# Fewer PE instructions, larger weight loads, one store, and one load split by partition halves in a cached-attention and GEGLU kernel

## The chip, the cores and the metric

The kernel runs on one core of one Trainium2 chip. The metric is the device time of one execution in microseconds (us), the median of several. One execution of one experiment (e17) was in a slower state, 209.65 us against 191.32 to 191.49 for the other three of that kernel; all times compared below are of fast executions. Where 2% is called faster, same or slower, fast runs alone are used, with a 95% interval.

## The reference

A single token per sequence (B = 2, D = 640) goes through a layer norm with a modulation computed from `c`, attention of 32 heads of 192 over the last 1024 of 4096 cached keys, and a GEGLU feed-forward of width 1536. All arrays are bf16.

```python
mod = (silu(c) @ w_mod).reshape(2, 6, 1, 640)          # sa, ca, ga, sb, cb, gb
h = layernorm(x) * (1 + ca) + sa
q = (h @ wq).reshape(B, 1, 32, 192)                    # wq 640 x 6144
k, v = k_cache[:, :, 3072:], v_cache[:, :, 3072:]      # B x 32 x 1024 x 192 each
x = x + ga * (softmax(q @ k.T * 192**-0.5) @ v).reshape(B, 1, 6144) @ wo
h = layernorm(x) * (1 + cb) + sb
x = x + gb * ((gelu(h @ w_gate) * (h @ w_up)) @ w_down)  # w_down 1536 x 640
```

## The kernel before

It is a stream of loads: nearly 77 MB pass through SBUF once, and compute follows. `w_mod` comes first, then `wq`, the key and value groups and `wo` through a ring of eight slots; then `w_gate`, `w_up` and `w_down` go into the place where `w_mod` was. All large loads are issued by SyncE on one queue (`q1` of the page below, 76.88 MB). The parts that matter here are the score reduction, the tail's loads, the feed-forward and the end.

```python
KPS = SLOT // NQ                        # wq in 5 pieces of one k-tile
WD_SPLIT = [(0, 2), (2, 1), (3, 1)]     # w_down in 3 pieces
# ... score reduction: 12 chunks of 16 columns, N = 256 each
for t in range(NCH):
    last = e.matmul(o_ap, lhsT=ident_b[:, :], rhs=prod[:, pz, :, t * GC:(t + 1) * GC], ...)
# ... the loads of the tail
S.dma("sp", k_dma(wg_v..., B_w_gate...), sem_wg, ...)
S.dma("sp", k_dma(wu_v..., B_w_up...), sem_wu, ...)
wd_src = B_w_down.rearrange("(a p r) n -> p a (r n)", a=FA, r=FR)
for ci, (a0, na) in enumerate(WD_SPLIT):
    S.dma("sp", k_dma(wd_v[:, a0 * FR:(a0 + na) * FR, :]..., wd_src[:, a0:a0 + na, :]), sem_wd[ci], ...)
# ... gate and up: the weights are the stationary operand, 60 matmuls of 2 columns each
for fc in range(FC):
    for k in range(KT):
        last = e.matmul(ps[:, bk, fc * 2:fc * 2 + 2], lhsT=wv[:, k, ...][:, :, r], rhs=h2T[:, k, :], ...)
# ... down, one function per piece of w_down; then the end
for b in range(B):
    S.dma(("sp", "act")[b], k_dma(out[b, 0, :]..., finb[b:P:32, :]), sem_out[b], ...)
with nc.Block() as block:
    ...                                 # each engine's list is emitted inside the block
```

Of the kernel before, what the change touches and what calls it, by code (L numbers as in the profile page):

```python
# [5 lines left out]
ALU = mybir.AluOpType  # L6
# [8 lines left out]
class _Op:  # L15
    __slots__ = ("eng", "fn", "name", "deps", "sem", "val", "inc")

    def __init__(self, eng, fn, name):
        self.eng = eng
        self.fn = fn  # L20
        self.name = name
        self.deps = []
        self.sem = None
        self.val = None
        self.inc = 1


class _Sched:

    def __init__(self, nc, es):  # L30
        self.nc = nc
        self.es = es
        self.lists = {k: [] for k in _COMPUTE + ("sp",)}
        self.counter = {k: es.enter_context(nc.semaphore("cnt_" + k)) for k in _COMPUTE}
        self.bufs = {}
        self.dma_uses = {}
        self.ncount = {k: 0 for k in _COMPUTE}

# [20 lines left out]
    def op(self, eng, fn, reads=(), writes=(), name="", deps=()):  # L59
        o = _Op(eng, fn, name)  # L60
        self._track(o, reads, writes, deps)
        self.lists[eng].append(o)
        self.ncount[eng] += 1
        o.sem = self.counter[eng]
        o.val = self.ncount[eng]
        return o

    def dma(self, eng, fn, sem, reads=(), writes=(), name="", deps=()):
# [7 lines left out]
        self.lists[eng].append(o)  # L76
        return o

    def emit(self, engname, eng, tail=None):
        waited = {}  # L80
        cnt = 0
        for o in self.lists[engname]:
            need = {}
            for d in o.deps:
                if d.eng == "pe" and engname == "pe" and d.inc == 1:
                    continue
                key = d.sem.num
                if need.get(key, (None, 0))[1] < d.val:
                    need[key] = (d.sem, d.val)
            for key, (s, v) in need.items():  # L90
                if waited.get(key, 0) >= v:
                    continue
                eng.wait_ge(s, v)
                waited[key] = v
# [9 lines left out]
def bass_adaLN_cond__sliding_block_cached__geglu_ffn__decode_kernel(  # L104
# [31 lines left out]
    FA, FR = 4, 3  # L136
    FC = F // P
    assert B == 2 and D == KT * P and J * PH == W and NQD * HQ == H and NT * P == NQ
    assert DD * NT == Dh and DD * H == P and FA * FR == FC and FC * P == F and DR == KT * 32
# [5 lines left out]
    GC = 512 // J  # L145
# [7 lines left out]
    KPS = SLOT // NQ  # L153
    NWQ = -(-KT // KPS)
    TPS = SLOT // D
    WO_SPLIT = []
    while sum(n for _, n in WO_SPLIT) < NT:
        t0 = sum(n for _, n in WO_SPLIT)
        WO_SPLIT.append((t0, min(TPS, NT - t0)))
    NWO = len(WO_SPLIT)  # L160
    WD_SPLIT = [(0, 2), (2, 1), (3, 1)]
    X0 = HQ * DD * (NQD - 1) + DD - 1
    ZW = X0 + P + 1
    QW = 2 * Dh
    NQB = NQ // (NR * QW)
    MH = 3 * DR

    es = ExitStack()
    with es:
# [11 lines left out]
        qbc = sb("qbc", [P, B, NQD, Dh], BF16)  # L181
# [6 lines left out]
        mneg = sb("mneg", [P, HQ], BF16)  # L188
# [8 lines left out]
        scT = sb("scT", [P, KT, B], BF16)  # L197
# [16 lines left out]
        nmx = sb("nmx", [1, 2, HQ], F32)  # L214
# [3 lines left out]
        On = sb("On", [P, 2, ON], BF16)  # L218
        oT = sb("oT", [P, NT, B], BF16)
        gl = sb("gl", [P, FC, B], F32)  # L220
        aT = sb("aT", [P, FC, B], BF16)
# [14 lines left out]
        sem_x = [S.sem("d_x%d" % b) for b in range(B)]  # L236
# [3 lines left out]
        sem_wu = S.sem("d_wu")  # L240
        sem_wd = [S.sem("d_wd%d" % i) for i in range(len(WD_SPLIT))]
        sem_ring = [S.sem("d_ring%d" % i) for i in range(NS)]
        sem_out = [S.sem("d_out%d" % b) for b in range(B)]
# [10 lines left out]
        slot_of = {it: n % NS for n, it in enumerate(items)}  # L254
        ring_state = {"next": 0, "done": set()}

# [3 lines left out]
        def ring_src(it):  # L260
            kind, i = it
            if kind == "wq":
                k0, k1 = i * KPS, min(KT, (i + 1) * KPS)
                return A_wq.rearrange("(p k) n -> p (k n)", k=KT)[:, k0 * NQ:k1 * NQ], (k1 - k0) * NQ
# [5 lines left out]
            return src[b, quad * HQ:(quad + 1) * HQ, K0:Sk, :].rearrange("h (p j) d -> p h (j d)", p=PH), SLOT  # L270

        def declare_ring(consumed=()):
            ring_state["done"].update(consumed)
            while ring_state["next"] < len(items):
                n = ring_state["next"]
                if n >= NS and items[n - NS] not in ring_state["done"]:
                    break
                slot = n % NS
                src, width = ring_src(items[n])
                S.dma("sp", k_dma(ring[:, slot, 0:width], src), sem_ring[slot], writes=[("ring", slot)], name="ld_%s%d" % items[n])  # L280
# [7 lines left out]
        xz = S.bufs["xr"][0]  # L288
        for b in range(B):
            S.dma("act", k_dma(xr[b:P:32, :], A_x[b, 0, :].rearrange("(i n) -> i n", i=NR)), sem_x[b], writes=[("xr", b)], deps=[xz], name="ld_x%d" % b)  # L290
# [8 lines left out]
        S.op("pool", lambda e: e.affine_select(out=selrow[:, :, :], in_=ones_b[:, 0:1].unsqueeze(2).broadcast_to([P, NR, B]),  # L299
                                                pattern=[[-32, NR], [-1, B]],  # L300
                                                compare_op=ALU.is_equal, fill=0.0, base=0, channel_multiplier=1),
             reads=["ones_b"], writes=["selrow"], name="selrow")
# [11 lines left out]
        S.op("pool", lambda e: e.memset(zsel[:, :, :], 0.0), writes=["zsel"], name="zsel0")  # L314

# [13 lines left out]
        def c_T(e):  # L329
            last = None  # L330
            for j in range(KT):
# [3 lines left out]
        S.op("act", lambda e: e.activation(out=scT[:, :, :], in_=c_ps[:, :, :], func=ACTF.Silu),  # L335
             reads=[bank(BK_T)], writes=["scT"], name="silu")
        S.op("dve", lambda e: e.tensor_copy(out=X[:, :], in_=xr[:, :]),
             reads=["xr"] + [("xr", b) for b in range(B)], writes=["X"], name="x_f32")
# [20 lines left out]
        def ln_mod(tag, opc_idx, s_idx, dst_bf):  # L359
# [7 lines left out]
            def f(e):  # L367
# [12 lines left out]
        S.op("dve", lambda e: e.tensor_scalar(out=mneg[:, :], in0=mask_h[:, :], scalar1=-1.0, scalar2=NEG, op0=ALU.add, op1=ALU.mult),  # L380
             reads=["mask_h"], writes=["mneg"], name="mneg")
# [3 lines left out]
        S.op("dve", lambda e: e.tensor_reduce(out=zsel[:, :, X0:X0 + DD * HQ].rearrange("p q (h d) -> p q h d", d=DD)[:, :, :, 0],  # L385
# [4 lines left out]
        for half in range(2):  # L390
            def f(e, half=half):
                last = None
                for k in range(KT):
                    wv = wm_v[:, k, :].rearrange("p (m i n) -> p m i n", i=NR, n=DR)
                    for i in range(NR):
                        last = e.matmul(ps[32 * i:32 * i + B, half, 0:MH].rearrange("p (m n) -> p m n", n=DR), lhsT=scT[:, k, :],  # L396
# [11 lines left out]

        for w in range(NWQ):
            def f(e, w=w):  # L410
                last = None
                for k in range(w * KPS, min(KT, (w + 1) * KPS)):
                    wv = ring[:, slot_of[("wq", w)], (k - w * KPS) * NQ:(k - w * KPS + 1) * NQ].rearrange("p (q h d) -> p q h d", h=NR, d=Dh)
                    for n in range(NQB):
                        for i in range(NR):
                            last = e.matmul(ps[32 * i:32 * i + B, n, 0:QW].rearrange("p (q d) -> p q d", d=Dh), lhsT=hT[:, k, :],  # L416
                                            rhs=wv[:, 2 * n:2 * n + 2, i, :],
                                            start=(k == 0), stop=(k == KT - 1), tile_position=(0, 32 * i))
                return last
            S.op("pe", f, reads=["ln1_out", ("ring", slot_of[("wq", w)])], writes=[bank(n) for n in range(NQB)], name="q1_%d" % w)  # L420
            declare_ring([("wq", w)])
        for n in range(NQB):
            if n % 2 == 0:
                S.op("act", lambda e, n=n: e.activation(out=qrow[:, n * QW:(n + 1) * QW], in_=ps[:, n, 0:QW], func=ACTF.Copy),
                     reads=[bank(n)], writes=[("qrow", n)], name="q1_evac%d" % n)
            else:
                S.op("dve", lambda e, n=n: e.tensor_copy(out=qrow[:, n * QW:(n + 1) * QW], in_=ps[:, n, 0:QW]),  # L427
                     reads=[bank(n)], writes=[("qrow", n)], name="q1_evac%d" % n)
        for u, (n, b) in enumerate((n, b) for n in range(NQB) for b in range(B)):
            bk = BK_T + u % 4  # L430
            S.op("pe", lambda e, n=n, b=b, bk=bk: e.matmul(ps[:, bk, 0:QW], lhsT=selq[:, b, :], rhs=qrow[:, n * QW:(n + 1) * QW], start=True, stop=True),
                 reads=[("selq", b), ("qrow", n)], writes=[bank(bk)], name="q2_%d_%d" % (n, b))
            S.op("act", lambda e, n=n, b=b, bk=bk: e.activation(out=qbc[:, b, 2 * n:2 * n + 2, :].rearrange("p q d -> p (q d)"),  # L433
                                                                in_=ps[:, bk, 0:QW], func=ACTF.Copy),
                 reads=[bank(bk)], writes=[("qbc", b, 2 * n), ("qbc", b, 2 * n + 1)], name="q2_evac%d_%d" % (n, b))
        S.op("dve", lambda e: e.memset(ps[:, 5:8, :], 0.0), writes=[bank(k) for k in range(5, 8)], name="init_O2")  # L436

        def d_mul(g, ci):
# [4 lines left out]
                                                  in1=qbc[:, b, quad, :].unsqueeze(1).broadcast_to([P, JC, Dh]), op=ALU.mult),  # L443
                 reads=[("ring", sl), ("qbc", b, quad)], writes=[("prod", 2 * (g % 2) + ci)], name="mul%d_%d" % (g, ci))

        def p_reduce(g, ci):
            bk = g % 2
            pz = 2 * (g % 2) + ci

            def f(e):  # L450
                last = None
                o_ap = ps[:, bk, ci * JC * GC:(ci + 1) * JC * GC].rearrange("p (j c) -> p j c", c=GC)
                for t in range(NCH):
                    last = e.matmul(o_ap, lhsT=ident_b[:, :], rhs=prod[:, pz, :, t * GC:(t + 1) * GC],  # L454
                                    start=(ci == 0 and t == 0), stop=(t == NCH - 1), skip_group_check=True)
                return last
            S.op("pe", f, reads=[("prod", 2 * (g % 2) + ci), "ident_b"], writes=[bank(bk)], name="red%d_%d" % (g, ci))

        def c_sum(g):
            z = g % 2  # L460
            S.op("dve", lambda e: e.tensor_reduce(out=S_sb[:, z, :], in_=ps[:, z, :].rearrange("p (j c) -> p j c", c=GC),  # L461
                                                  axis=AX.X, op=ALU.add),
                 reads=[bank(z)], writes=[("S", z)], name="sum_%d" % g)
# [5 lines left out]
        def c_max2(g):  # L469
            z = g % 2  # L470
            S.op("dve", lambda e: e.tensor_reduce(out=nmx[:, z, :], in_=ps[0:1, BK_T, 0:P].rearrange("p (x h) -> p h x", h=HQ),  # L471
                                                  axis=AX.X, op=ALU.max, negate=True),
                 reads=[bank(BK_T)], writes=[("nmx", z)], name="max2_%d" % g)

        def c_bc(g):
            z = g % 2

            def f(e):
                o_ap = ps[:, BK_T, P:P + HQ]
                e.matmul(o_ap, lhsT=ones_f[0:1, :], rhs=nmx[:, z, :], start=True, stop=False)  # L480
                return e.matmul(o_ap, lhsT=ident_b[:, :], rhs=mneg[:, :], start=False, stop=True)  # L481
# [207 lines left out]
```

## Time and profile before

| | before |
|---|---|
| time, median of 3 runs | 192.12 us |
| span of the profiled run | 190.5 us |
| bytes loaded | 76.88 MB |
| PE matmuls | 1401 |
| 16 KB instruction fetches in the DMA records | 11 |

The page's busy line and its slices say what bounds the kernel. PE is TensorE with its matmuls, PEld its weight loads, DVE is VectorE, ACT ScalarE, POOL GpSimd; x counts instructions. A digit is the busy share of one of 40 slices in tenths; the last line is what the DMA engines moved.

```profile
PE 109.4 (57%) x1401; PEld 74.3 (39%) x1401; DVE 88.7 (47%) x147; ACT 29.2 (15%) x74; POOL 3.0 (2%) x14
...
DMA  7999999999999999999999999999999999999960
GB/s 259 388 416 441 423 427 428 418 436 426 418 429 426 421 427 425 421 428 424 423 426 431 418 423 434 419 421 431 428 416 434 420 423 424 426 421 432 399 252 8
...
q1 hardware_dynamic: 7192, 76.88, 96.0%
q8 instruction: 11, 0.18, 0.4%
```

No compute engine is busy over 57%; the load queue is busy 96.0% of the time that 16 engines have, at 416 to 441 GB/s from the third slice to the 37th. So in the body the DMA rate alone counts, and most of what is left to gain lies in the head and the tail. The `q8` line is easily overlooked: these are the fetches of instructions (11 of 16 KB), and the profile counts them on the same 16 engines.

Next the windows of the tail. The columns are the window in us and its length, then the busy time (and count) of PE, PEld, DVE, ACT and POOL, the granted PE clock, the DMA share of the 16 engines, and GB/s.

```profile
178.00:180.00 2.00, 1.76 (x60) 1.73 (x60) 0.17 (x1) 0.00 (x0) 0.00 (x0) 0.50 0.95 392
180.00:182.00 2.00, 0.27 (x9) 0.22 (x8) 0.00 (x0) 0.19 (x1) 0.00 (x0) 0.50 1.04 410
182.00:183.00 1.00, 1.00 (x43) 1.00 (x41) 0.00 (x0) 0.00 (x0) 0.00 (x0) 0.50 0.92 361
183.00:184.00 1.00, 0.60 (x22) 0.51 (x19) 0.18 (x1) 0.00 (x0) 0.00 (x0) 0.50 0.63 257
184.00:185.00 1.00, 0.43 (x16) 0.46 (x20) 0.00 (x0) 0.00 (x0) 0.00 (x0) 0.50 0.30 123
185.00:186.00 1.00, 0.89 (x30) 0.42 (x20) 0.00 (x0) 0.00 (x0) 0.00 (x0) 0.50 0.19 66
186.00:187.00 1.00, 0.40 (x16) 0.19 (x12) 0.00 (x0) 0.00 (x0) 0.00 (x0) 0.50 0.02 8
```

The share falls from 0.92 to 0.02 over five windows: the 16 engines don't end together. The last load has 16 completions in the records. The records carry no engine numbers; a completion is read here as one engine's. The first comes at 183.13 and the last at 186.77, a spread of 3.64 us. Work of the kernel's end waits for the slowest engine, as the end of the chain of waits shows (start in us, duration, what):

```profile
156.72 30.05 DMA r<-in_B_w_down_dram
186.77 0.04 issue
186.81 0.60 PE ps L625 x12
187.41 0.02 issue
187.44 0.33 DVE fin L630
```

After the last piece of `w_down` only 12 matmuls, two DVE operations and the store are left.

### The profile page before, as it was taken

The page shows a single profiled execution, that of the slowest core. Times are in us where ns is not written, and L with a number is a line of the kernel's source. Part 1 is how long each engine was busy: PE and PEld are TensorE (multiplying, and loading weights), DVE is VectorE, ACT ScalarE, POOL GpSimd, SP SyncE. Part 2 cuts the span into 40 slices and gives each one's busy share as a digit, 9 for nine tenths or more (in the row PEclk, how much of TensorE's full clock was granted, in tenths as well). Part 3 has the DMA queues.
Part 4 walks back from the last instruction along what each step waited for, and adds up shares of the span by engine and source line. Part 5 has one row for each costly group of instructions (what it writes and reads, how often), then busy time and mean ns, then how long its engine had stood idle before and what let it go on. Part 6 is the DMA issues. An engine that isn't in the chain of part 4 may idle for free.

```text
span 190.5 us, 3243 instructions
## 1 busy us (share of the span) xinstructions
PE 109.4 (57%) x1401; PEld 74.3 (39%) x1401; DVE 88.7 (47%) x147; ACT 29.2 (15%) x74; POOL 3.0 (2%) x14
## 2 busy tenths in 40 slices
PE   0014853628678773674689656646759856224452
PEld 0011310105556552462457444434536624223450
DVE  6123000248699549458477476485495620003201
ACT  3031100370022101011011011012010230003400
POOL 6000000000000000000000000000000000000000
PEclk9999999999999999999957999999975995555555
DMA  7999999999999999999999999999999999999960
GB/s 259 388 416 441 423 427 428 418 436 426 418 429 426 421 427 425 421 428 424 423 426 431 418 423 434 419 421 431 428 416 434 420 423 424 426 421 432 399 252 8
DMA packets 7234, 77.09 MB, mean 405 GB/s; under 512 B 818, under 2 KB 820, under 8 KB 1460
## 3 DMA queue, kind: packets, MB, share of 16 engines
q1 hardware_dynamic: 7192, 76.88, 96.0%
q8 instruction: 11, 0.18, 0.4%
q14 instruction: 3, 0.02, 0.0%
q10 hardware_dynamic: 28, 0.01, 0.0%
HBM read 76.88 MB, written 0.00 MB: 404 GB/s over the span
## 4 chain that ended last, share of the span: by engine, by line
DMA 71%; DVE 13%; SPq 5%; PE 4%; issue 3%; ACT 2%
DMA ring<-in_A_k_cache_dram 39%; DMA ring<-in_A_wq_dram 16%; DMA r<-in_B_w_down_dram 16%; DVE prod L441 8%; SPq L246 5%; PE ps L454 3%; DVE S_sb L461 2%; ACT qbc L433 2%; PE ps L416 1%; DVE ps L436 1%; DVE M L464 1%; PE ps L480 0%; DVE rden L516 0%; PE ps L625 0%; DVE Sb_sb L486 0%
## 5 line engine op out<-in xcount | busy, mean ns | idle before, releaser
L441 DVE TENSOR_TENSOR prod<-ring,qbc 128x3072 bf16<-128x3072 bf16 x32 | 55.9, 1752 | 21.7 <-DMA ring<-in_A_k_cache_dram 21.7
L454 PE MATMUL ps<-prod,ident_b 128*128 128x256 bf16 x384 | 53.4, 296 | 21.0 <-DVE prod L441 21.0
L454 PEld LDWEIGHTS ps<-prod,ident_b 128*128 128x128 bf16 x384 | 38.2, 105 | 33.1 <-DVE prod L441 25.4
L518 ACT ACTIVATE On<-ps,rden 128x384 bf16<-128x384 f32 x16 | 9.3, 580 | 46.5 <-DVE rden L516 33.1
L480 PE MATMUL ps<-nmx,ones_f 1*128 1x4 f32 x32 | 6.5, 271 | 15.2 <-DVE nmx L471 15.2
L506 PE MATMUL ps<-ring,E_sb 128*8 128x384 bf16 x256 | 13.6, 334 | 0.0
L489 ACT ACTIVATE E_sb<-Sb_sb 128x128 bf16<-128x128 f32 x16 | 5.0, 309 | 53.3 <-DVE Sb_sb L486 53.3
L480 PEld LDWEIGHTS ps<-nmx,ones_f 1*128 1x128 f32 x32 | 5.1, 198 | 20.3 <-DVE nmx L471 20.3
L575 PE MATMUL ps<-ring,oT 128*2 128x160 bf16 x192 | 7.2, 333 | 8.3 <-DMA ring<-in_A_wo_dram 7.8
L461 DVE TENSOR_REDUCE S_sb<-ps 128x32 f32<-128x512 f32 x16 | 10.8, 673 | 1.7 <-PE ps L454 1.7
L416 PE MATMUL ps<-ring,hT 128*2 128x384 bf16 x80 | 7.1, 516 | 7.5 <-DMA ring<-in_A_wq_dram 6.7
L486 DVE TENSOR_TENSOR Sb_sb<-S_sb,ps 128x128 f32<-128x128 f32 x16 | 4.6, 288 | 10.7 <-PE ps L481 10.7
L575 PEld LDWEIGHTS ps<-ring,oT 128*2 128x2 bf16 x192 | 5.4, 115 | 9.9 <-DMA ring<-in_A_wo_dram 9.3
L592 DVE TENSOR_TENSOR lnt<-ps,modR 128x160 f32<-128x160 f32 x1 | 0.3, 324 | 17.5 <-PE ps L575 17.5
L345 PE MATMUL ps<-st,selstat 128*128 128x2 f32 x4 | 1.1, 349 | 11.2 <-ACT sqj L341 11.2
L427 DVE CAST qrow<-ps 128x384 bf16<-128x384 f32 x2 | 1.0, 553 | 13.7 <-PE ps L416 13.7
L416 PEld LDWEIGHTS ps<-ring,hT 128*2 128x2 bf16 x80 | 2.1, 108 | 12.6 <-DMA ring<-in_A_wq_dram 8.9
L530 PEld LDWEIGHTS ps<-On,zsel 128*128 128x128 bf16 x128 | 6.1, 110 | 1.2 <-ACT On L518 1.2
L530 PE MATMUL ps<-On,zsel 128*128 128x48 bf16 x128 | 6.0, 187 | 0.8 <-ACT On L518 0.8
L506 PEld LDWEIGHTS ps<-ring,E_sb 128*8 128x8 bf16 x256 | 4.9, 86 | 3.0 <-issue 0.5
L495 PEld LDWEIGHTS ps<-denp,maskc 128*128 128x128 f32 x32 | 5.3, 209 | 1.2 <-ACT E_sb L489 1.0
L396 PE MATMUL ps<-r,scT 128*2 128x480 bf16 x40 | 4.3, 596 | 2.1 <-DMA r<-in_w_mod_dram 2.1
(71 smaller groups left out, 74.9 us busy)
## 6 DMA issues: line engine op xcount, KB each, us to landing
ring<-in_A_k_cache_dram SPq DMA_DIRECT2D x16, 1536.0 KB, 25.1
ring<-in_A_v_cache_dram SPq DMA_DIRECT2D x16, 1536.0 KB, 25.6
ring<-in_A_wq_dram SPq DMA_DIRECT2D x5, 1536.0 KB, 23.9
ring<-in_A_wo_dram SPq DMA_DIRECT2D x5, 1440.0 KB, 24.7
r<-in_w_mod_dram SPq DMA_DIRECT2D x1, 4800.0 KB, 14.2
r<-in_B_w_gate_dram SPq DMA_DIRECT2D x1, 1920.0 KB, 26.9
r<-in_B_w_up_dram SPq DMA_DIRECT2D x1, 1920.0 KB, 31.0
r<-in_B_w_down_dram SPq DMA_DIRECT2D x1, 960.0 KB, 33.3
```

What stands on the lines that cost most here:

```text
L246: return lambda e: e.dma_start(dst, src)
L416: last = e.matmul(ps[32 * i:32 * i + B, n, 0:QW].rearrange("p (q d) -> p q d", d=Dh), lhsT=hT[:, k, :], rhs=wv[:, 2 * n:2 * n + 2, i, :], ...
L441: S.op("dve", lambda e: e.tensor_tensor(out=prod[:, 2 * (g % 2) + ci, :, :], in0=ring[:, sl, ci * JC * Dh:(ci + 1) * JC * Dh].rearrange("p ...
L454: last = e.matmul(o_ap, lhsT=ident_b[:, :], rhs=prod[:, pz, :, t * GC:(t + 1) * GC], start=(ci == 0 and t == 0), stop=(t == NCH - 1), skip ...
L461: S.op("dve", lambda e: e.tensor_reduce(out=S_sb[:, z, :], in_=ps[:, z, :].rearrange("p (j c) -> p j c", c=GC), axis=AX.X, op=ALU.add), re ...
L480: e.matmul(o_ap, lhsT=ones_f[0:1, :], rhs=nmx[:, z, :], start=True, stop=False)
L489: S.op("act", lambda e: e.activation(out=E_sb[:, z, :, :], in_=Sb_sb[:, z, :, :], func=ACTF.Exp, scale=SCALE, accum_out=denp[:, z:z + 1]), ...
L495: S.op("pe", lambda e: e.matmul(ps[:, BK_T, P + 16:P + 17], lhsT=maskc[:, :], rhs=denp[:, z:z + 1], start=True, stop=True), reads=[("denp" ...
L506: last = e.matmul(ps[32 * i:32 * i + 2 * HQ, BK_O, 0:ON], lhsT=E_sb[:, z, 2 * jp:2 * jp + 2, :].rearrange("p j h -> p (j h)"), rhs=ring[:, ...
L518: S.op("act", lambda e: e.activation(out=On[:, z, :], in_=ps[:, BK_O, 0:ON], func=ACTF.Identity, scale=rden[:, z:z + 1]), reads=[bank(BK_O ...
L530: last = e.matmul(ps[:, BK_OT, b * NT:(b + 1) * NT], lhsT=zsel[:, jj, x:x + P], rhs=On[:, z, jj * Dh + dd * NT:jj * Dh + (dd + 1) * NT], s ...
L575: last = e.matmul(ps[32 * i:32 * i + B, BK_M, 0:DR], lhsT=oT[:, t, :], rhs=wv[:, tl, i, :], start=(t == 0), stop=(t == NT - 1), tile_posit ...
```

## The change

The intent is to even out the tail and to shorten what surrounds it. PE gets fewer instructions (1049 matmuls for 1401), so that fewer instruction fetches (11 in the records before) fall on the DMA engines: the score reduction works on 32 columns at a time (N = 512, 192 matmuls for 384), gate and up take the weights as the moving operand (50 for 120), and the selection matmuls halve. `wq` comes in two loads for five, `wo` in three for six, `w_up` in two for one. There is one store for two, and no block around the emission. Last, the three-row piece of `w_down` is split: the lower 64 partitions come by a load with a pattern that gave it eight completions, the upper 64 by one with 16, so as to give eight engines more bytes than the others.

```diff
-    GC = 512 // J
+    GC = 512 // JC
...
+    WQ_SPLIT = [(0, 2), (2, 3)]
+    WO_SPLIT = [(0, 28), (28, 17), (45, 3)]
+    WU_SPLIT = [(0, 3), (3, 2)]
-    WD_SPLIT = [(0, 2), (2, 1), (3, 1)]
+    WD_SPLIT = [(9, 3), (0, 5), (5, 3), (8, 1)]
...
-            return src[b, quad * HQ:(quad + 1) * HQ, K0:Sk, :].rearrange("h (p j) d -> p h (j d)", p=PH), SLOT
+            return src[b].rearrange("(i u) s d -> u i s d", u=NQD)[quad, :, K0:Sk, :].rearrange("i (p j) d -> p i (j d)", p=PH), SLOT
...
-        wd_src = B_w_down.rearrange("(a p r) n -> p a (r n)", a=FA, r=FR)
+        wd_src = B_w_down.rearrange("(p r) n -> p (r n)", r=FC)
+        for ci, (r0, nr) in enumerate(WD_SPLIT):
+            dst, src = wd_v[:, r0:r0 + nr, :].rearrange("p r n -> p (r n)"), wd_src[:, r0 * D:(r0 + nr) * D]
+            if r0 >= FC - FR:
+                S.dma("sp", k_dma(dst[0:HP, :], src[0:HP, :].rearrange("(m e) n -> e m n", e=8)), sem_wd[ci], ...)
+                S.dma("sp", k_dma(dst[HP:P, :], src[HP:P, :]), sem_wdh, ...)
+            else:
+                S.dma("sp", k_dma(dst, src), sem_wd[ci], ...)
...
-        for b in range(B):
-            S.dma(("sp", "act")[b], k_dma(out[b, 0, :].rearrange("(i n) -> i n", i=NR), finb[b:P:32, :]), sem_out[b], ...)
-        with nc.Block() as block:
...
+        S.dma("sp", k_dma(out[:, 0, :].rearrange("b (i n) -> i b n", i=NR), finb[0:P:RB, :]), sem_out, ...)
+        S.resolve()
+        S.emit("sp", nc.sync, tail=lambda e: e.wait_ge(sem_out, 16))
+        ...                                # the other four engines alike
```

## The prediction

> **What bounds the kernel now.** DMA. The page's queue table gives 76.88 MB on one queue, 96.0% of the 16 engines' span; the slices show 416 to 441 GB/s from the third to the 37th, with PE, DVE and ACT busy 57%, 47% and 15%. What remains is the head (first packet 1.8 us in, unchanged) and the tail. The windows give a DMA share of 0.92, 0.63, 0.30, 0.19, 0.02 for the microseconds from 182 to 187: with balanced engines the bytes would be in by about 184.1, but the last w_down piece lands at 186.81 (chain of waits); then 12 matmuls 0.60, two DVE operations 0.68, stores, end at 190.5.
>
> **Why the engines are uneven.** The DMA records hold 11 instruction fetches of 16 KB, about 1.06 us each, on one engine each, one per some 256 PE instructions. [...]the 16 completions of the last load fall into seven at 183.1 to 183.8, seven at 184.6 to 185.2, and two at 186.4 and 186.8.
>
> **What the change does.**
> 1. PE matmuls 1401 to about 1049 (reduction 384 to 192, selection 128 to 64, gate and up 120 to 50, 12 transposes added). At two instructions each: 8 fetches, not 11, fewer engines hit twice. Per hit I estimate 1.4 us from the gap between the groups.
> 2. Half of three w_down rows (245 KB) on eight engines. [...]the records carry no engine numbers. 15 KB more on each low engine and less on each other: 0.58 us each way at the recorded 26.5 bytes/ns. Right if fetches fall on the high engines.
> 3. Larger wq and wo pieces: 11.5 to 12 KB packets run at 26.5 bytes/ns, the 38 KB ones of w_mod at 27.0: about 0.4 us on 15.7 MB.
> 4. One store, no block end: the barrier after the last store takes 0.35 us, and the SP store landed 0.27 us after the ACT one. About 0.5 us together.
>
> The last load should land near 184.2. But then PE is next: wo comes in three coarse pieces (end +0.3 us); gate and up, 2 x 5 x 384 columns at the 363 ns per round of four that wq shows, are again 1.8 us each; geglu grows from 24 to 384 columns (+0.35), plus transposes and copy (0.8), then 48 matmuls at 38 ns. This chain reaches the final DVE operation near 185.3, against 187.44: 2.1 gained there, 0.5 at the end.
>
> **Predicted: 189.3 us** against 192.12 (-1.5%), range 187.9 to 190.8. Faster by over 2%: 0.21; within 2%: 0.77; slower: 0.02.
>
> **What would show it.** Eight 16 KB fetches; the 16 completions of the last load within 1.5 us; last landing at 184 to 185; the down matmuls' last wait on DVE rather than DMA; slices unchanged at 420 to 436 GB/s; span end 0.35 us nearer the store's landing.
>
> **What would make it wrong.** The eighth fetch falling on a loaded engine in the last 3 us (+1.4); fetches on the low engines (+0.6); gate and up slowed by 6-byte runs of the moving operand; KV heads 12.6 MB apart, not 1.6, moving the KV rate (1% is 1.2 us).

The sum stands at 2.1 us gained up to the final DVE operation and 0.5 at the end, 2.6 of the 2.8 between 192.12 and 189.3. "Low" and "high" engines are there no more than the eight that would carry the extra bytes and the others. The 1.4 us per hit, and that fewer engines would be hit twice, are estimates.

The figures behind it, from the traces of the two kernels: 11 fetches for 2802 PE and PEld instructions before, one per 255, and 8 for 2098 after, one per 262. Packets of 12 KB took 462 ns (median, 26.6 bytes/ns), those of 11.5 KB 435 (26.5), those of 38 KB 1420 (27.0). The 363 ns are four rounds of `wq` matmuls in 1.45 us before; the 38 ns are 36 `wo` matmuls in 1.37 us. The multiplication after GELU took 0.18 us with 24 columns before and 0.56 with 384 after; the transposes and their copy 0.47 and 0.20 after. The stores before landed at 189.80 and 190.07, and the last instruction of the block's end began 0.36 us after that. For the 0.3 us of `wo` the text gives no source.

## The result

The change takes 191.38 us (191.28 to 191.69, four runs), against 192.06 for the kernel before beside it. The ratio is 0.9969, with a 95% interval of 0.9952 to 0.9986: within 2%. A ratio here is always the mean time of one kernel's fast runs over that of the other's fast runs of the same rounds, so it is not quite the ratio of the medians quoted. The time lies above the predicted range, which ended at 190.8.

The page after, the same lines:

```profile
PE 108.7 (57%) x1049; PEld 53.2 (28%) x1049; DVE 98.1 (52%) x147; ACT 29.9 (16%) x72; POOL 5.1 (3%) x23
...
DMA  7899998999999999999999999999999999999990
GB/s 259 389 461 419 419 485 365 432 429 422 427 435 417 430 423 421 427 429 420 424 427 424 429 423 422 426 432 419 429 420 424 484 400 431 417 418 411 324 293 33
...
q1 hardware_dynamic: 6500, 76.88, 97.1%
q8 instruction: 8, 0.13, 0.3%
```

The matmuls and the fetches are as planned: 1049 and 8. The share of `q1` rose from 96.0% to 97.1% for the same 76.88 MB, which alone tells little: e1 below has 97.0% and is 2.4 us faster. But the last three slices move 324, 293 and 33 GB/s, together no more than the 399, 252 and 8 before: the tail drags. The windows show where:

```profile
176.00:178.00 2.00, 1.91 (x25) 1.10 (x25) 0.00 (x0) 0.03 (x1) 0.00 (x0) 0.50 1.02 416
178.00:180.00 2.00, 1.22 (x15) 0.55 (x15) 0.00 (x0) 0.47 (x1) 0.00 (x0) 0.50 1.05 247
180.00:182.00 2.00, 0.64 (x10) 0.27 (x10) 0.00 (x0) 0.00 (x0) 0.00 (x0) 0.87 1.03 241
182.00:183.00 1.00, 0.25 (x4) 0.03 (x2) 0.56 (x1) 0.00 (x0) 0.00 (x0) 1.00 1.07 285
183.00:184.00 1.00, 0.50 (x16) 0.44 (x20) 0.20 (x1) 0.00 (x0) 0.00 (x0) 0.97 0.88 303
184.00:185.00 1.00, 0.53 (x12) 0.20 (x12) 0.00 (x0) 0.00 (x0) 0.00 (x0) 0.50 0.94 365
185.00:186.00 1.00, 0.40 (x16) 0.40 (x20) 0.00 (x0) 0.00 (x0) 0.00 (x0) 0.50 0.52 201
186.00:187.00 1.00, 0.68 (x26) 0.35 (x16) 0.00 (x0) 0.00 (x0) 0.00 (x0) 0.50 0.09 32
```

Read the last two columns together. From 178 to 182 the DMA share is 1.03 to 1.05, so no engine idles; yet the rate is 241 to 247 GB/s, against 392 to 410 before. The engines are busy with slow packets. The share alone hides it. The single DMA records say the same: between 178 and 182 a packet of 3840 B took 264 ns on average, one of 6400 B 424 ns and one of 6144 B 408 ns, while in the same kernel between 176 and 177.5 one of 6144 B took 237 ns, and after 184 one of 3840 B took 151 and one of 6400 B 248. All sizes are slowed by about 1.7, those of whole loads of `w_up` and of the five-row piece too, and not only those of the two half loads. It begins at about 177.9, shortly after the first packets of the half loads (from 177.57), and ends at about 183.5, as the last completions of these loads come (183.09 to 183.82).

The end of the chain after:

```profile
153.62 33.11 DMA r<-in_B_w_down_dram
186.72 0.04 issue
186.77 0.75 PE ps L697 x14
187.51 0.02 issue
187.54 0.34 DVE fin L702
```

The last two DVE operations (`fin`, then `finb`) start at 187.54, where they started at 187.44 before. Until the tail the change was well ahead: the last completion of `w_gate` came at 175.28 (177.14 before), and its 16 completions were spread by 1.86 us, not 3.38. All of that was given back in five microseconds. What remains of the gain is the end: from the final DVE operation to the end of the span there are 2.5 us, before 3.1 (190.0 less 187.54, 190.5 less 187.44).

### The profile page after: what moved, and what is told of

It is laid out like the page before. It is cut to its first block, busy times and chain, and to the rows that moved or that the text cites. A ratio compares the mean times of both kernels' runs of the same rounds, so it can differ in the third digit from the quotient of the medians.

```text
span 190.0 us, 2430 instructions
## 1 busy us (share of the span) xinstructions
PE 108.7 (57%) x1049; PEld 53.2 (28%) x1049; DVE 98.1 (52%) x147; ACT 29.9 (16%) x72; POOL 5.1 (3%) x23
## 3 DMA queue, kind: packets, MB, share of 16 engines
q1 hardware_dynamic: 6500, 76.88, 97.1%
HBM read 76.88 MB, written 0.00 MB: 405 GB/s over the span
## 4 chain that ended last, share of the span: by engine, by line
DMA 71%; DVE 15%; PE 7%; ACT 2%; SPq 2%; issue 1%
DMA ring<-in_A_k_cache_dram 36%; DMA r<-in_B_w_down_dram 17%; DMA ring<-in_A_wq_dram 17%; DVE prod L491 9%; PE ps L503 4%; DVE S_sb L510 4%; SPq L267 2%; PE ps L468 2%; ACT qbc L484 2%; DVE ps L486 1%; DVE M L513 1%; ACT qrow L475 1%; PE ps L527 0%; DVE bcR L520 0%; PE ps L697 0%
## 5 line engine op out<-in xcount | busy, mean ns | idle before, releaser
L503 PE MATMUL ps<-prod,ident_b 128*128 128x512 bf16 x192 | 54.0, 426 | 13.5 <-DVE prod L491 13.5
L503 PEld LDWEIGHTS ps<-prod,ident_b 128*128 128x128 bf16 x192 | 17.7, 105 | 39.4 <-DVE prod L491 16.9
L510 DVE TENSOR_REDUCE S_sb<-ps 128x32 f32<-128x1024 f32 x16 | 19.3, 1206 | 2.1 <-PE ps L503 2.1
L527 PE MATMUL ps<-bcR,bcL 5*128 5x4 f32 x32 | 6.4, 266 | 20.4 <-DVE bcR L520 20.4
L468 PE MATMUL ps<-ring,hT 128*2 128x512 bf16 x60 | 6.3, 592 | 10.1 <-DMA ring<-in_A_wq_dram 9.1
L527 PEld LDWEIGHTS ps<-bcR,bcL 5*128 5x128 f32 x32 | 4.9, 192 | 25.1 <-DVE bcR L520 25.1
L623 PE MATMUL ps<-ring,oT 128*17 128x160 bf16 x192 | 6.1, 313 | 7.5 <-DMA ring<-in_A_wo_dram 7.5
L623 PEld LDWEIGHTS ps<-ring,oT 128*17 128x17 bf16 x192 | 5.4, 124 | 8.0 <-DMA ring<-in_A_wo_dram 8.0
L446 PE MATMUL ps<-r,scT 128*17 128x480 bf16 x40 | 4.3, 597 | 3.3 <-DMA r<-in_w_mod_dram 3.3
L541 PE MATMUL ps<-denp,maskc 128*128 128x1 f32 x32 | 5.1, 230 | 0.8 <-ACT E_sb L535 0.8
```

The costliest lines, as they stand in the source:

```text
L446: last = e.matmul(ps[32 * i:32 * i + RM, half, 0:MH].rearrange("p (m n) -> p m n", n=DR), lhsT=scT[:, k, :], rhs=wv[:, 3 * half:3 * half + ...
L468: last = e.matmul(ps[32 * i:32 * i + B, n, :], lhsT=hT[:, k, :], rhs=wv[:, kk, i, n * QW:(n + 1) * QW], start=(k == 0), stop=(k == KT - 1) ...
L510: S.op("dve", lambda e: e.tensor_reduce(out=S_sb[:, z, :], in_=ps[:, 2 * z:2 * z + 2, :].rearrange("p k (j c) -> p (k j) c", c=GC), axis=A ...
L527: S.op("pe", lambda e: e.matmul(ps[:, BK_T, P:P + HQ], lhsT=bcL[:, :], rhs=bcR[:, z, :], start=True, stop=True), reads=[("bcR", z), "bcL"] ...
L541: S.op("pe", lambda e: e.matmul(ps[:, BK_T, P + 16:P + 17], lhsT=maskc[:, :], rhs=denp[:, z:z + 1], start=True, stop=True), reads=[("denp" ...
L623: last = e.matmul(ps[32 * i:32 * i + RM, BK_M, 0:DR], lhsT=oT[:, t, :], rhs=wv[:, tl, i, :], start=(t == 0), stop=(t == NT - 1), tile_posi ...
```

## The experiments

Eighteen kernels ran, all with correct results. "Confined" below is a load of only the lower or only the upper 64 partitions. The time of 3840 B packets is a mean, for packets that started between 178 and 182 us (for e12 between 182 and 186, the slow stretch of that kernel), from the DMA records; the engine count of a load is read from the number of its completions in the records, counted after its issue. The kernel before, run beside each group of experiments, took 192.02 to 192.19 us, so differences of 0.2 us between experiments of different groups are not resolved.

| run | what it is | us | ratio to before | 3840 B packets, ns |
|---|---|---|---|---|
| after | split: lower 64 on 8 engines, upper 64 on 16 | 191.38 | 0.9969 | 264 |
| e1_plain | one load of 128 partitions | 188.95 | 0.9838 | 152 |
| e2_half16 | lower 64, upper 64, both on 16 | 191.45 | 0.9963 | 252 |
| e3_low8_rows | meant as 8 engines, was 16 | 191.28 | 0.9967 | 245 |
| e4_low8_two32 | 32, 32 and 64 partitions, was 16 engines | 191.43 | 0.9970 | 286 |
| e5_even_rows | halves, fed from even and odd rows | 191.24 | 0.9946 | 262 |
| e6_even_parts | even partitions, odd partitions | 188.99 | 0.9837 | 152 |
| e9_low8_even | meant as e6 on 8 engines, was 16 | 188.87 | 0.9833 | 152 |
| e13_low8_spread | even partitions on 8 engines, odd on 16 | 190.59 | 0.9919 | 221 |
| e14_spread_few | e13 with 25 fewer matmuls | 190.77 | 0.9928 | 257 |
| e16_extra_low8 | e1 and an extra lower half on 8 engines | 191.70 | 0.9979 | 242 |
| e17_extra_up16 | e1 and an extra upper half on 16 engines | 191.48 | 0.9961 | no fast trace |
| e18_eight_strided | eight loads of every eighth partition | 191.25 | 0.9957 | 263 |
| e12_before_half | the kernel before, one load split in halves | 194.26 | 1.0117 | 256 |
| e7_small_chunks | e1 with wq in 5 loads and wo in 6 | 189.58 | 0.9869 | 152 |
| e8_more_pe | e1 and 384 idle matmuls | 190.16 | 0.9897 | 152 |
| e10_few_pe | e1 with 51 fewer matmuls | 188.96 | 0.9838 | 152 |
| e15_block | e1 in a block | 189.85 | 0.9877 | 152 |
| e11_block_stores | e1 in a block, two stores | 190.02 | 0.9901 | 152 |

### Which part of the change does it: e1

The theory was that the split of the three-row piece slows the tail. The rivals were the rest of the change: the new gate and up, the coarser loads, the order of the pieces. The edit takes only the split out (with the column order of gate and up that belonged to it):

```diff
-                S.dma("sp", k_dma(dst[0:HP, :], src[0:HP, :].rearrange("(m e) n -> e m n", e=8)), sem_wd[ci], ...)
-                S.dma("sp", k_dma(dst[HP:P, :], src[HP:P, :]), sem_wdh, ...)
+                S.dma("sp", k_dma(dst, src), sem_wd[ci], ...)
```

> The changed kernel with its three w_down rows loaded by one plain 128-partition load on 16 engines. Theory (the half loads cause the 5.7 us, from 177.8 to 183.5, in which 3840-byte packets took 263 ns instead of 150): no such window, packets 150 ns throughout, last w_down landing near 184.5 instead of 187.1, time near 189.0 us. Rival (the slow window comes from something else of the change, such as the gate and up matmuls reading the weights in 6-byte runs while the loads write): the window stays and the time stays at 191.4.

It took 188.95 us, 2.4 less than the change. Its windows:

```profile
178.00:180.00 2.00, 1.21 (x15) 0.48 (x15) 0.00 (x0) 0.11 (x1) 0.00 (x0) 1.00 1.02 415
180.00:182.00 2.00, 1.02 (x16) 0.44 (x17) 0.56 (x1) 0.00 (x0) 0.00 (x0) 1.00 1.01 410
182.00:183.00 1.00, 0.70 (x24) 0.40 (x21) 0.20 (x1) 0.00 (x0) 0.00 (x0) 1.00 0.86 326
183.00:184.00 1.00, 0.52 (x20) 0.32 (x20) 0.00 (x0) 0.00 (x0) 0.00 (x0) 1.00 0.44 170
184.00:185.00 1.00, 0.46 (x16) 0.25 (x16) 0.00 (x0) 0.00 (x0) 0.00 (x0) 0.90 0.04 15
```

The share is what it was in the changed kernel, about 1.0, but the rate is 410 to 415 where that one had 241 to 247. The tail then falls off in three windows, not five. The slow stretch is large enough for the loss: from 177.9 to 183.4 the DMA records of the changed kernel hold 1.40 MB, and 412 GB/s would have moved 2.27. By an estimate the missing 0.87 MB take 2.1 us, most of the 2.4. And the end of the chain of e1:

```profile
152.88 31.61 DMA r<-in_B_w_down_dram
184.49 0.04 issue
184.54 0.39 PE ps L695 x12
184.92 0.01 issue
184.93 0.34 PE ps L695 x3
185.27 0.02 issue
185.29 0.34 DVE fin L700
```

The final DVE operation starts at 185.29, 2.25 us earlier than after the change. The split is the cause of the loss, and the rest of the change, taken together, is a gain. It also shows that the last step still follows a landing: the chain runs through the DMA, not through DVE.

### Is it the eight engines, the source, or the destination: e2 to e6, e9

One theory was the eight-engine load; another that rows read out of one half of the piece collide in memory; a third that the destination does it.

```diff
 e2:
-                S.dma("sp", k_dma(dst, src), sem_wd[ci], ...)
+                S.dma("sp", k_dma(dst[0:HP, :], src[0:HP, :]), sem_wd[ci], ...)
+                S.dma("sp", k_dma(dst[HP:P, :], src[HP:P, :]), sem_wdh, ...)
 e3: as e2, with the lower source as src[0:HP, :].rearrange("(e m) n -> e m n", e=8)
 e4: as e3, with the lower 64 partitions as two loads of 32
 e5: as e2, with sources src[0:P:2, :] and src[1:P:2, :] (and gate and up columns to match)
 e6: dst[0:P:2, :] from src[0:P:2, :], and dst[1:P:2, :] from src[1:P:2, :]
 e9: as e6, with the even source as .rearrange("(e m) n -> e m n", e=8)
```

> As the changed kernel, but the lower 64 partitions of the three rows are loaded by a plain load (16 engines, rows in order), the upper 64 as before. If any load that writes only 64 partitions makes engines collide at the destination: slow window stays in part or whole, 3840-byte packets near 260 ns, time 190.5 to 191.4. If the eight-engine load or the permuted rows cause it: no slow window, time near 189.0.

> As the changed kernel[...]. If the permuted order of the source rows slows the reads: no slow window, near 188.6 to 189.0. If the number of engines or the destination is the cause: unchanged, 191.4 with 3840-byte packets at 263 ns.

> [...]If two engines meeting at one group of partitions is the cause[...]: the packets of the lower half return to about 150 ns and at most the upper half, on 16 engines, stays slow; time 189 to 190. If an eight-engine load is slow whatever it writes: 191.4 as before.

> Two 64-partition loads on 16 engines as in e2_half16, same destinations (lower and upper 64 partitions), but the first reads the even rows and the second the odd rows of w_down, so each reads over the whole matrix. If reading one half of the rows in memory is what slows: no slow window, near 189.0 us. If the destination (64 partitions) is: as e2_half16, 3840-byte packets near 260 ns, 191.0 to 191.5.

> Two 64-partition loads on 16 engines, one to the even and one to the odd partitions, rows in natural order, so each load spreads over all partitions. If it is the confinement to one half of the partitions that makes engines collide: faster than e2_half16, toward 189.0 us. If any load of 64 partitions is dealt to engines in another way than a load of 128 and so collides: slow window stays, 190.5 to 191.5.

> The balancing of the change without its confinement: [...]By e6_even_parts no slow window. If the engines that run late are the high ones: spread of the last load down from 2.0 us toward 1, last landing up to 0.5 us earlier, 188.4 to 188.8. If they are the low ones, or a mixture: spread 2.5 to 3.2, time 189.0 to 189.6. If an eight-engine load collides even when spread: 3840-byte packets above 200 ns, 190 or more.

e2 is as slow as the change, 191.45 us, with 16 completions in both halves: eight engines are not needed for it. e5 keeps the confined destination but reads from all over the piece, and stays slow at 191.24. e6 keeps two loads on the same 16 engines, the same packets, and only interleaves the partitions:

```profile
178.00:180.00 2.00, 1.70 (x25) 0.82 (x16) 0.00 (x0) 0.49 (x1) 0.00 (x0) 0.72 1.03 418
180.00:182.00 2.00, 1.16 (x21) 0.57 (x22) 0.56 (x1) 0.00 (x0) 0.00 (x0) 1.00 1.01 409
```

The rate is that of e1, and the time too, 188.99. e5 and e6 read the same rows in two loads each and differ in the destination, with the gate and up columns that go with it. So, among loads on 16 engines, neither the number of loads, nor the size of the packets, nor the source, but the set of destination partitions decides.

e3, e4 and e9 are misses. They were meant to run on eight engines, but had 16 completions, while the load of the change had eight. What the records show is this much: the loads with the source order `(m e)` (the change, e13) had eight completions, those with `(e m)` (e3, e4, e9) had 16. Which engines these are, and which rows or partitions an engine takes, they don't show; the passages of the recorded texts that said so are cut (e3, e4, e9, and e13 below). "High" and "low" in e9 and e13 are, as in the prediction, only names for the engines without and with the extra bytes. So e3 is e2 again, e9 is e6 again, and e4 shows that two loads of 32 partitions do no better than one of 64 (3840 B packets of 286 ns on average, up to 496).

### Does it depend on this kernel: e12

```diff
+            if ci == 1:
+                S.dma("sp", k_dma(dst[0:64], wd_src[0:64, a0:a0 + na, :]), sem_wd[ci], ...)
+                S.dma("sp", k_dma(dst[64:P], wd_src[64:P, a0:a0 + na, :]), sem_wdh, ...)
```

> The kernel before with one change: its second w_down piece (three rows of each of 128 partitions) loaded as the lower and the upper 64 partitions, each on 16 engines. If confining a load to one half of the partitions slows all loads in flight, it does so here too: 3840-byte packets at 250 ns or more for some 4 us and 1.0 to 2.2 us more, 193 to 194.3. If it takes something else of the change to bring it about: 192.1.

The kernel before, with nothing but its second piece of `w_down` in halves, took 194.26 us, 2.24 more than the kernel before beside it. Its windows:

```profile
182.00:183.00 1.00, 0.62 (x23) 0.63 (x24) 0.00 (x0) 0.00 (x0) 0.00 (x0) 0.50 1.02 238
183.00:184.00 1.00, 1.00 (x43) 1.00 (x40) 0.00 (x0) 0.00 (x0) 0.00 (x0) 0.50 1.01 223
```

Where the unsplit kernel moved 361 in the first of these, this one moves 238 with the share at 1.02. The same penalty comes without any other part of the change.

### What about the destination: e13, e14, e16 to e18

e5 against e6 says that the destination partitions decide, and not what it is about them. In the slow windows of the changed kernel, of e2 and of e12 all engines together moved 223 to 256 GB/s; with the same rows by even and odd partitions (e6) they moved 409 to 418, and in one load (e1) 410 to 415. The theory tested here is confinement: a load whose partitions lie in one contiguous half slows all packets in flight. Two more theories rested on statements about the hardware that no run here shows. They are cut from the recorded texts of e16 to e18, with the expectations that followed from them alone; of the "three theories" and "the others" that are still named there, confinement is the one that remains. It has e16 and e17 slow and e18 fast.

```diff
 e13: as e6, with the even source as .rearrange("(m e) n -> e m n", e=8) (and columns to match)
 e14: as e13, with bf16 shifts and three transposes for twelve
 e16: e1 and
+                S.dma("sp", k_dma(prod[0:HP, 0, 0:10, :]..., src[0:HP, :].rearrange("(m e) n -> e m n", e=8)), sem_wdh, ...)
 e17: e1 and
+                S.dma("sp", k_dma(prod[HP:P, 0, 0:10, :]..., src[HP:P, :]), sem_wdh, ...)
 e18: e1 with the three rows as
+                for z in range(8):
+                    S.dma("sp", k_dma(dst[z:P:8, :], src[z:P:8, :]), sem_w8[z], ...)
```

> A load [...]as in the change, but over the even partitions (the loads of e3, e4 and e9 showed 16 completions[...]). No confinement, so 3840-byte packets near 150 ns. If the eight engines that finish first are the low ones: the two groups of completions (182.7 to 183.7 and 184.2 to 184.8) close up, last landing near 184.3, 188.3 to 188.6. If early and late engines are mixed over low and high: last landing 184.8 to 185.4, 189.0 to 189.6. If an eight-engine load slows the others by itself: packets over 200 ns, 190.5 or more.

> e13_low8_spread with 25 matmuls less (3 transposes for 12, bf16 shift). If the balancing works and the eighth fetch costs nothing: as e13_low8_spread within 0.15 us. If the fetch, now about 50 instructions later in the program, falls on an engine still loading: up to 0.5 us slower or faster.

> The kernel with the plain three-row load, plus one more load issued just before it: the lower 64 partitions of the same three rows, with the pattern of the changed kernel that runs on eight engines, into a buffer that is dead by then. It isolates the eight-engine lower half. Three theories. Confinement: any load that lies in one contiguous half of the partitions slows all packets in flight. [...]packets of 3840 B at 220 to 280 ns and under 320 GB/s for some 2 to 5 us from about 178. [...]Time: 245 KB more are 0.6 us at 415 GB/s, and put on eight engines 1.2 us: [...]191 or more under the others.

> As the run before, but the extra load is the upper 64 partitions on 16 engines, the other of the changed kernel's two loads. [...]All three theories: slow, packets of 3840 B at 220 to 280 ns, under 320 GB/s for some 2 to 5 us, and a time of 190.5 or more. If it is at 152 ns, all three fall.

> The three rows in eight loads of 16 partitions, each with every eighth partition (z, z+8, ...), [...]the same 128 packets of 3840 B in all. Each load spans both halves of the partitions[...]. [...]confinement: 152 ns, over 400 GB/s, 189.0 to 189.4 (six more semaphore writes per engine at about 10 ns, and some 3 us more of issuing, which lies far ahead of the landing).

e18 was made to decide. Its loads each span the whole range of partitions, and none is confined. Its windows:

```profile
178.00:180.00 2.00, 1.44 (x19) 0.55 (x15) 0.00 (x0) 0.49 (x1) 0.00 (x0) 0.50 1.03 233
180.00:182.00 2.00, 0.43 (x10) 0.27 (x10) 0.00 (x0) 0.00 (x0) 0.00 (x0) 0.88 1.04 242
```

It is as slow as the halves: 233 to 242 GB/s, 191.25 us. If its partitions are what slows it, the contiguous half is not what matters: every eighth partition is slow, every second (e6) is not. Why, no run shows. e18 also issues eight loads, not two; but all eight were issued by 157 us, some 21 us before the slow stretch. (For the "about 10 ns" of its expectation: the 732 4-byte records of the load queue took 9.4 ns on average after the change.) What was not tested is whether eight loads as small as these (16 partitions, those of e6 have 64) are slow whatever partitions they have: that confinement falls rests on this run alone.

e16 shows that the eight-engine lower half is slow by itself: from 178 to 182 the rate is 267 to 268 GB/s in its windows, and packets of 3840 B average 224 to 267 ns in each microsecond. It doesn't tell its partitions from its eight engines as the reason (e13). By an estimate from e1, 245 KB more should take it to about 189.6 at 415 GB/s, or to 190.1 with all of it on eight engines at 26.5 bytes/ns; it took 191.70. e17's profile fell into a slow execution of 209.65 us, so its trace can't be compared with the others; within it, 3840 B packets took 345 ns between 192.5 and 194, as the engines came to the extra load, and 150 after 197. Its three fast runs, 191.32 to 191.49, lie 1.7 to 1.9 us above the 189.6, slow as expected. So either half of the changed kernel's split is slow by itself, the upper one by its time and by a slow trace only.

e13 is the one version in which the idea itself, more bytes for eight engines, ran without confinement. Its eight-engine load had eight completions, and 3840 B packets took 221 ns: slower than 152, faster than the halves. From 178 to 182 all engines moved 293 to 300 GB/s. In e14, with the same split, such packets took 257 ns, as slow as the halves. Among the completions of the last load of e13, eleven of 16 came within one microsecond (184.67 to 185.64), in e1 at most eight; but all 16 were spread over 3.06 us (e1 2.07), the mean came 1.2 us later than in e1 (184.96 against 183.77) and the last at 186.31. So whether the shift evens out the engines is hidden by the slow packets. Against e6 the eight engines, with the order of the source rows that brings them about, cost 1.6 us (e13) and 1.8 us (e14): a second way to slow the packets in flight, of which no run here shows the reason. e14 hoped to win by moving the eighth fetch and gained nothing (190.77).

### What the other parts are worth: e7, e8, e10, e11, e15

```diff
 e7:
-    WQ_SPLIT = [(0, 2), (2, 3)]
-    WO_SPLIT = [(0, 28), (28, 17), (45, 3)]
+    WQ_SPLIT = [(k, 1) for k in range(KT)]
+    WO_SPLIT = [(t, min(9, NT - t)) for t in range(0, NT, 9)]
 e8: 12 matmuls of 2 columns added after each half of a score reduction, results unused
+                for _ in range(12):
+                    last = e.matmul(ps[0:2, BK_M, 500:502], lhsT=ident_b[:, 0:2], rhs=ident_b[:, 0:2], ...)
 e10: bf16 shift and denominators, three transposes for twelve, gate and up without the extra split
 e15: with nc.Block() around the emission
 e11: as e15, and two stores, on SyncE and ScalarE, as before
```

> e1_plain with the small wq and wo pieces of the kernel before (five of 12 KB and five of 11.5 KB plus one per partition). By the packet rates the large pieces are worth about 0.4 us of transfer: 189.3 to 189.4. If large pieces are worth nothing, or the finer arrival helps PE: 189.0 or less.

> e1_plain with 384 idle two-column matmuls added in the attention, 768 PE instructions, so 11 instruction fetches instead of 8 with those of the tail at the same places of the program. If fetches delay the engines that carry them: mean completion of the last w_down load +0.2 to +0.3 us, its spread larger, time +0.2 to +1.4 (189.2 to 190.4). If fetches are hidden and the instruction count alone does not matter: 188.95.

> e1_plain with 51 matmuls less (one gate and one up matmul per row group and k, 3 transposes instead of 12, bf16 instead of two-pass f32 for the shift and the denominators), 102 PE instructions less, so that the eighth instruction fetch comes at the very end or not at all. If that fetch still costs time in e1_plain: 188.3 to 188.7. If it falls on an engine that has done its share: 188.8 to 189.0.

> e1_plain with the two stores and the block end of the kernel before. My prediction booked 0.5 us for both together: 189.4 to 189.5. If the final barrier hides behind other work of the program's end: 189.0.

> e1_plain with the block end of the kernel before, but one store. e11_block_stores cost 1.07 us where I had booked 0.5; 0.57 of it lay between the last DVE operation and the end of the span, and the time exceeded the span by 1.75 us instead of 1.25. If the block makes both: 189.7 to 189.9, time minus span 1.75. If the second store makes the part outside the span: 189.3, time minus span 1.25.

- e7: small loads cost 0.6 us (189.58 against 188.95). In the profiled runs the mean engine completes the last load at 184.21, in e1 at 183.77. The packets of the smaller pieces ran at 26.4 to 26.5 bytes/ns, those of the larger ones in e1 at 26.8 to 27.0 (12 to 37 KB each).
- e8: 384 idle matmuls, 768 instructions, brought the fetches from 8 back to 11 and cost 1.2 us. The spread of the last load went from 2.07 to 3.34 us, its mean by 0.29 only. PE is busy 55% of the span in e1, so it had room for them; what moved with the time are the fetches and the spread.
- e10: 51 fewer matmuls (the shift and the denominators in f32 have 32 matmul records each in e1, in bf16 16 each here; 10 fewer of gate and up, nine fewer transposes) moved the eighth fetch from 182.7 to 184.4 and gained nothing. The count stayed at 8: where this one falls cost nothing.
- e15 and e11: the block costs 0.7 to 0.9 us (by ratios or by medians), of which about half lies within the span (188.2 for 187.8) and the rest outside of it: the time less the span is 1.75 us with a block and 1.25 without. The second store is worth 0.2 to 0.5 us more (by medians or by ratios), not well resolved.

### The best version

e1_plain, e6, e9 and e10 are equal within their intervals at 188.9 to 189.0 us: a ratio of 0.984 to the kernel before, and 1.3% under the change (188.95 over 191.38). The one to keep is e1_plain: the whole change without the split.

## Why the prediction was wrong

The time was predicted at 189.3 and came to 191.38. The step that failed is its item 2: "Half of three w_down rows (245 KB) on eight engines", costed as "15 KB more on each low engine and less on each other: 0.58 us each way at the recorded 26.5 bytes/ns". That treats the split as a shift of bytes between engines whose rates stay as they are. What the runs showed in its place: the rates don't stay. While engines work on either half, packets in flight take about 1.7 times as long on average, for 5.5 us, and the split costs 2.4 us (e1), in the kernel before too (2.2, e12). Spread over all partitions, the same shift onto eight engines still slows the packets (221 ns in e13, 257 in e14, for 152) and costs 1.6 to 1.8 us: there too the rates didn't stay. With the split taken out, the remaining change stands at 188.95, inside the predicted range.

The other steps, one by one:

- Fetches, right in number (8) and in kind: with three more of them the engines end 3.34 us apart, not 2.07, and the kernel takes 1.2 us more (e8). In this kernel, whose load queue is busy 97.0% of the time of 16 engines (e1), three more fetches (one took 1.07 us on average before, 1.06 after) cost 1.2 us, 0.4 each on average.
- The spread of the last load's completions, predicted within 1.5 us: 2.61 after the change, 2.07 in e1. Eight fetches still go with more spread than I allowed for.
- Last landing at 184 to 185: 187.13 after the change, 184.88 in e1.
- Final DVE operation at 185.3: 187.54 after, 185.29 in e1, but the match is luck, and not for my reason. I had PE as the next limit; in e1 the chain still runs through the landing of `w_down`.
- Larger pieces, 0.4 us: 0.6 (e7). Right in kind, undersized: 15.7 MB over 16 engines at the prediction's own 26.5 and 27.0 bytes/ns differ by nearly 0.7 us, by an estimate.
- The end, 0.5 us: 1.1 (e11). Undersized. I read 0.35 us of barrier in the span; about as much again lies outside the span, where the trace doesn't show it.
- Worries that did not come true: the farther key and value heads did not lower the rate (a turn of the eight slots took 29.5 us in both kernels), and gate and up by the moving operand hold nothing up (after, PE waited 2.1 us there for `w_up`).

From before to e1 there are 3.1 us. The pieces measured on e1 are 1.1 (block and stores), 0.6 (larger loads) and 1.2 (fetches), 2.9 in all; the 0.2 left are within the error of such a sum, and that the pieces simply add was not tested. The split takes 2.4 of the 3.1 back, and 0.7 remain.

What is settled: the split is the cause (e1, e12), and on 16 engines its destination partitions are (e5 against e6). Every load confined to one half was slow (after, e2 to e5, e12, e16, e17, the last by its time and a slow trace), and so were the eight loads of every eighth partition (e18); the 16-engine loads to all partitions or to every second one were not (e1, e6, e9). What is not settled is why: the records show neither engine numbers nor anything of the destination, so no mechanism is shown. That the contiguous half is not what matters rests on e18, and why e13 and e14, with the even partitions on eight engines, are slow is open.

## What to carry to other kernels

Don't split a load by partition halves (or, as e18 suggests, into loads of every eighth partition) in a kernel that DMA bounds: here it slowed the other loads in flight (packets of 6400 B from 248 to 424 ns), and a DMA share of 1.03 to 1.05 hid it, so read GB/s beside the share. If a load has to be split, split it by even and odd partitions: that was free here on 16 engines (188.99 us for 188.95), and not on eight (190.59). Where DMA is the limit, as here, PE instructions can cost through their fetches even when PE has room (e8: three fetches and 1.2 us more), and what comes after the last store costs too (e15: 0.7 to 0.9 us).
